# Loading the real weights of one spectral mode in eight pieces instead of one transfer

## The chip, the cores and the metric

The kernel runs on one core of a Trainium2 chip. The metric is the device time of one execution in microseconds (us), the median of several. The core has five engines that run side by side, each with its own queue of instructions: PE (matmuls, with PEld for its weight loads), DVE (vector work), ACT (scalar work, activations), POOL and SP. Data come from HBM through 16 DMA engines, which all queues share.

## What is computed

A sparse attention is followed by a spectral mix. The second part is where the change lies:

```python
x = attention(q, k, v)                     # (8, 576, 512)
X = np.fft.rfft(x, axis=1)                 # 64 modes of it are kept
Yr = einsum('bmd,mde->bme', Xr, w_r) - einsum('bmd,mde->bme', Xi, w_i)
Yi = einsum('bmd,mde->bme', Xr, w_i) + einsum('bmd,mde->bme', Xi, w_r)
y = np.fft.irfft(Y, n=576, axis=1)
u = x + y
out = u + np.maximum(u @ w_ch, 0.0)
```

`w_r` and `w_i` are (64, 512, 512) in float32, 134 MB together. Every weight is used once, for a batch of 8, so the kernel has to bring all of them in from HBM, and it casts them to float16 on the way.

## The kernel before

**Stages.** The attention runs first, strided heads and then local heads. The Fourier transform of x is a matmul with a table (`dft`). The modes are done in two rounds of 64: `mode(slot, m)` works on one half of the 512 input channels, `half = 1 - slot`: round 0 takes the half of the strided heads, beside the local attention, and round 1 that of the local heads, beside the channel mix of x itself (`turn` and `premix`). `mode` does 16 small matmuls (line 547): the stationary operand is a 128 by 128 block of weights, the moving one 16 columns, 8 batches times real and imaginary. The 128 partitions hold 64 rows of the real weights (partitions 0 to 63) over 64 rows of the imaginary ones (64 to 127), so a mode can't start before both of its parts are in.

**The weights.** `w_fetch` (line 174) loads a pair of modes into one tile `wt` of shape [128, 2, 4, 512]: index 1 is the mode of the pair, and a partition's 4 x 512 values are 4 KB of float16 read from 8 KB of contiguous float32. For most pairs there are two transfers, 64 rows of the real part of both modes and 64 rows of the imaginary part, 512 KB each as written (line 196). For the last two pairs, `i >= 2 * NM - 4`, there is one transfer for each part of each mode, 256 KB (line 199), in the order real of the first, real of the second, imaginary of the first, imaginary of the second. The very last pair, `i == 2 * NM - 2` or 126, holds modes 62 and 63 of round 1. All these transfers are issued from POOL's queue, which also issued the loads of q, k and v at the start. Among those are loads of 72 rows that are split into 64 (lines 227 and 229) and 8 (line 231); line 231 is issued twelve times.

`w_fetch` is called at the end of every odd mode (line 555), when that mode's tile comes free: five buffers of the pool `pw` take turns. POOL does nothing else meanwhile. The framework gives the DMAs of POOL's queue eight semaphores in turn; the next DMA on a semaphore waits until the one before on it has landed.

**The order of work at the end.** The program is written out by hand, engine by engine in the order of the code (`manual_schedule`). Modes 0 to 53 of round 1 have turns and premixes between them (lines 845 to 855). Modes 54 to 63 (line 956) have only a few early matmuls, and then `again(n)`, matmuls whose result nobody uses, that keep PE busy between modes (line 949): four after modes 58 to 61, two after 62 and 63. The sums of modes 62 and 63 leave PSUM together, by the add of line 575 after mode 63. Then come `spec_last(0)` (lines 884 and 886, the channel mix of the last 16 modes), three more `again`, `spec_out` on ACT and DVE (lines 675, 677, 678; helper line 260), and the loop over 36 output units: `v_rows` and `u_rows` with the inverse transform (line 688), a ReLU on ACT (line 907), adds on POOL (line 909) and DVE (line 926), and the stores, mostly from SP's queue.

Of the kernel before, what the change touches and what calls it, by code (L numbers as in the profile page):

```python
# [19 lines left out]
NM = 64  # L20
# [59 lines left out]
def kernel(  # L80
# [10 lines left out]
    nc = tc.nc  # L91
# [82 lines left out]
    def w_fetch(n=1):  # L174
        for _ in range(n):
            i = len(w_tiles)
            if i >= 2 * NM:
                return
            half, m = 1 - i // NM, i % NM
            if i // 2 in GUEST:  # L180
                wt = big.tile([128, 2, 4, DM], F16, tag=GUEST[i // 2], name="wt")
            else:
                wt = pw.tile([128, 2, 4, DM], F16, tag="w", name="wt")
            for ri, src in enumerate((moe_w_r, moe_w_i)):
                dst = wt[ds(64 * ri, 64)]
                rows = src[m : m + 2, ds(256 * half, 256), :].rearrange(
                    "m (p c) e -> p m (c e)", c=4
                )
                dst = dst.rearrange("p m c e -> p m (c e)")


                ones = range(2)
                if ri and not m:
                    ones = [1]
                elif i < 2 * NM - 4:
                    nc.gpsimd.dma_start(dst, rows)  # L196
                    continue
                for j in ones:
                    nc.gpsimd.dma_start(dst[:, j], rows[:, j])
            w_tiles.extend((wt[:, 0], wt[:, 1]))  # L200

    def w_ch_fetch():
# [333 lines left out]
    def mode(slot, m):  # L536
# [17 lines left out]
        if m % 2 and (slot or m // 2 not in GUEST):  # L554
            w_fetch()
# [145 lines left out]
    const_load(nc.sync, "cMl", "cFl", "cA")  # L701
    load_str(2, 2)
    w_fetch()

    def str_front(b):
# [39 lines left out]
    for b in range(B):  # L745
        if b in (1, 3):
            load_str(b + 3, 2)
        load_loc(*[(), (), (), (), (0,), (1, 2), (3,), (4, 5)][b])
        w_fetch([2, 1, 1, 1, 1, 1, 0, 0][b])
        front = str_front(b + 1) if b + 1 < B else loc_front(0)  # L750
        for t in range(6):
            str_scores(b, t)
            if b > 0:
                if t < 2:
                    str_values(b - 1, 4 + t)
                elif t == 2:
                    dft(b - 1, 1)
            if t >= 2:
                str_values(b, t - 2)
            for w in front[SPLIT[t] : SPLIT[t + 1]]:  # L760
                w()
        if b == 1:
            nc.vector.memset(PL[:, 0:PS0], 0.0)
# [62 lines left out]
    for b in range(B + 1):  # L826
        for t in range(5):
            if b > 0:
                work.append(lambda b=b, t=t: premix(b - 1, t))
            if b < B and t < 4:  # L830
                half, cp = ((1, 0), (1, 1), (0, 0), (0, 1))[t]
# [181 lines left out]
```

## Time and profile before

| What | us |
|---|---|
| median of 3 runs | 434.96 |
| the runs | 434.02 to 435.61 |
| the profiled execution, one of the three | 435.61 |
| its span, from the first to the last instruction | 433.8 |

| Engine | busy us | share of the span |
|---|---|---|
| PE | 338.7 | 78% |
| PEld | 244.0 | 56% |
| DVE | 215.1 | 50% |
| ACT | 188.1 | 43% |
| POOL | 128.9 | 30% |

The page cuts the span into 40 slices of 10.8 us and gives the busy share of each in tenths. PEclk is the clock that PE was granted in tenths of full speed; DMA is the mean busy share of the 16 DMA engines. A list of queues says how many packets and bytes each moved. The chain of waits follows the work back from the last instruction to whatever released it. "issue" is time in which an engine waited for nothing that the profile shows. In the timeline a line has start and duration, engine, source line, operation, tiles and count, and in brackets how long the engine had been idle before and what ended that. The granted clock of the whole execution was 0.83.

By the list of DMA issues, a 512 KB transfer of weights lands 18.9 us (real) or 19.4 us (imaginary) after its issue in the median, and a 256 KB one 14.7 or 13.4 us after; a load of 8 rows by line 231 (64 KB, two packets a row) 11.5 to 12.2 us after.

### The profile page before, as it was taken

The page shows a single profiled execution, that of the slowest core. Times are in us where ns is not written, and L with a number is a line of the kernel's source. Part 1 is how long each engine was busy: PE and PEld are TensorE (multiplying, and loading weights), DVE is VectorE, ACT ScalarE, POOL GpSimd, SP SyncE. Part 2 cuts the span into 40 slices and gives each one's busy share as a digit, 9 for nine tenths or more (in the row PEclk, how much of TensorE's full clock was granted, in tenths as well). Part 3 has the DMA queues.
Part 4 walks back from the last instruction along what each step waited for, and adds up shares of the span by engine and source line. Part 5 has one row for each costly group of instructions (what it writes and reads, how often), then busy time and mean ns, then how long its engine had stood idle before and what let it go on. Part 6 is the DMA issues. An engine that isn't in the chain of part 4 may idle for free.

```text
span 433.8 us, 12099 instructions
## 1 busy us (share of the span) xinstructions
PE 338.7 (78%) x5307; PEld 244.0 (56%) x5307; DVE 215.1 (50%) x466; ACT 188.1 (43%) x353; POOL 128.9 (30%) x208
## 2 busy tenths in 40 slices
PE   1986888779886887889794566698669698977994
PEld 1865776657764665667663344465446465643441
DVE  2888678744523243342511033455346366503895
ACT  1686678635543435445340401133115122602892
POOL 6522332323232222222222222222222221200983
PEclk9999899869967659676855559868798899988999
DMA  8999999999999999999999999999999999991687
GB/s 178 212 213 213 215 212 212 212 210 213 215 212 214 213 214 213 213 214 214 213 213 213 213 213 215 213 213 215 213 213 213 214 213 213 214 179 29 260 331 275
DMA packets 28996, 92.18 MB, mean 212 GB/s; under 512 B 4048, under 2 KB 5072, under 8 KB 28944
## 3 DMA queue, kind: packets, MB, share of 16 engines
q0 software_dynamic: 24704, 81.28, 94.3%
q1 hardware_dynamic: 3440, 9.46, 5.8%
q10 hardware_dynamic: 800, 0.67, 0.6%
q8 instruction: 42, 0.69, 0.6%
q14 instruction: 10, 0.08, 0.0%
HBM read 163.22 MB, written 9.44 MB: 398 GB/s over the span
## 4 chain that ended last, share of the span: by engine, by line
DMA 69%; PE 18%; DVE 6%; ACT 3%; issue 2%; POOL 1%; DVEq 0%; POOLq 0%
DMA wt<-in_moe_w_i_dram 51%; DMA wt<-in_moe_w_r_dram 8%; DMA ring<-in_q_dram 5%; DMA w_ch<-in_moe_w_ch_dram 5%; DVE xb L250 2%; DVE kz L292 2%; PE y L547 2%; PE v L688 2%; PE u L688 2%; PE v L894 2%; PE sc L514 1%; ACT X L260 1%; DVE rec L249 1%; PE tp L395 1%; PE sc L353 1%
## 5 line engine op out<-in xcount | busy, mean ns | idle before, releaser
L547 PE MATMUL y<-X,wt 128*128 128x16 f16 (+1 forms) x2048 | 82.8, 192 | 59.5 <-DMA wt<-in_moe_w_i_dram 58.1
L547 PEld LDWEIGHTS <-wt 128*128 128x128 f16 (+1 forms) x2048 | 73.1, 103 | 75.4 <-issue 68.3
L196 POOL DMA_DIRECT2D wt<-in_moe_w_r_dram x62 | 36.4, 587 | 139.2 <-PE y L547 66.0
L196 POOL DMA_DIRECT2D wt<-in_moe_w_i_dram x60 | 35.2, 587 | 73.0 <-DMA wt<-in_moe_w_i_dram 60.2
L654 ACT ACTIVATE v<-sc 128x512 f16<-128x512 f32 x32 | 19.1, 596 | 68.4 <-PE sc L645 68.3
L471 ACT ACTIVATE PL<-sc 128x480 f16<-128x480 f32 (+1 forms) x48 | 27.7, 579 | 47.6 <-PE sc L457 46.9
L645 PE MATMUL sc<-w_cp,xT 128*128 128x512 f16 (+1 forms) x160 | 47.4, 424 | 0.0
L655 DVE COPY xo<-tp 128x512 f16<-128x512 f16 x32 | 22.1, 692 | 36.7 <-PE tp L653 36.4
L250 DVE TENSOR_TENSOR xb<-av,rec 90x256 f16<-90x256 f32 (+2 forms) x80 | 36.0, 450 | 2.8
L249 DVE RECIPROCAL rec<-av 90x4 f32<-90x4 f32 (+2 forms) x80 | 14.7, 183 | 45.3 <-PE av L486 33.9
L402 DVE COPY qT<-tp 128x576 f16<-128x576 f16 x16 | 12.0, 758 | 40.1 <-PE tp L395 37.2
L260 ACT ACTIVATE v<-tp 128x640 f16<-128x640 f16 (+1 forms) x24 | 19.4, 807 | 24.0 <-PE tp L429 21.1
L395 PE MATMUL tp<-cI_s,ring 64*64 64x64 f16 x864 | 26.4, 211 | 1.6 <-issue 0.8
L360 ACT ACTIVATE PL<-sc 90x360 f16<-90x360 f32 (+1 forms) x48 | 22.7, 490 | 6.2 <-PE sc L353 5.3
L926 DVE TENSOR_TENSOR osb<-u,rl 128x512 f32<-128x512 f32 x36 | 23.6, 689 | 3.3 <-ACT rl L907 1.7
L395 PEld LDWEIGHTS <-ring 64*64 64x64 f16 x864 | 20.7, 123 | 6.8 <-issue 3.6
L441 PE MATMUL sc<-cMl_s,cI_s 128*128 128x480 f16 (+1 forms) x48 | 23.0, 478 | 1.6 <-ACT X L260 1.6
L909 POOL TENSOR_TENSOR rl<-rl,xo 128x512 f32<-128x512 f32 x16 | 18.3, 1155 | 18.9 <-ACT rl L907 18.6
L457 PE MATMUL sc<-qT,kz 128*128 128x160 f16 (+1 forms) x160 | 23.4, 275 | 0.5 <-issue 0.5
L457 PEld LDWEIGHTS <-kz 128*128 128x128 f16 x160 | 16.8, 119 | 10.8 <-issue 8.1
L907 ACT ACTIVATE rl<-v 128x512 f32<-128x512 f32 x36 | 20.4, 597 | 4.9 <-PE v L688 4.2
L285 PE MATMUL tp<-cI_s,ring 72*128 72x72 f16 x256 | 15.1, 206 | 9.5 <-DMA ring<-in_v_dram 8.0
(103 smaller groups left out, 655.5 us busy)
## 6 DMA issues: line engine op xcount, KB each, us to landing
wt<-in_moe_w_r_dram POOLq DMA_DIRECT2D x62, 512.0 KB, 18.9
wt<-in_moe_w_i_dram POOLq DMA_DIRECT2D x60, 512.0 KB, 19.4
out_dram<-osb SPq DMA_DIRECT2D x14, 512.0 KB, 2.7
ring<-in_v_dram POOLq DMA_DIRECT2D x8, 288.0 KB, 13.4
ring<-in_q_dram POOLq DMA_DIRECT2D x8, 288.0 KB, 13.6
ring<-in_k_dram POOLq DMA_DIRECT2D x8, 288.0 KB, 13.0
ring<-in_v_dram POOLq DMA_DIRECT2D x3, 512.0 KB, 15.1
ring<-in_q_dram POOLq DMA_DIRECT2D x3, 512.0 KB, 14.8
```

The lines of the kernel that those rows point to most:

```text
L196: nc.gpsimd.dma_start(dst, rows)
L250: nc.vector.tensor_tensor(out=dst, in0=val.rearrange("p h (q c) -> p h c q", c=4), in1=rec[0:n, 0:pieces] .to_broadcast((n, pieces, 64)) . ...
L260: nc.scalar.activation(out=out, in_=in_, func=ACTF.Copy)
L360: nc.scalar.activation(out=PS[0:n, ds(POFF[t], 4 * n)], in_=scp[0:n, 0 : 4 * n], func=ACTF.Exp, scale=SCALE,)
L395: nc.tensor.transpose(tp[ds(64 * hp, 64), ds(64 * i, 64)], qn[ds(64 * hp, 64), ds(64 * (9 * g + i), 64)], idn[ds(64 * hp, 64), ds(64 * hp, ...
L441: nc.tensor.matmul(scp[:, 0 : n * times].rearrange("p (h x) -> p h x", h=times), idn, mask_rows("cMl", n, times), start=True, stop=False,)
L457: nc.tensor.matmul(scp[:, ds(col, n)], kzs[par][:, hp, ds(s0, 128)], qTs[par][:, ds(s0, n)], start=False, stop=(i == len(todo) - 1),)
L471: nc.scalar.activation(out=dst, in_=src, func=ACTF.Exp, scale=SCALE)
L547: nc.tensor.matmul(yv[:, mi, e, :], wt[pr, XC[c], ds(128 * e, 128)], Xh[half][pr, c, :, :, m], start=(c == 0), stop=(c == 3),)
L645: nc.tensor.matmul(vp[pr, :], xT[:, ch, cols], w_chs["cp"][:, ch, :], start=(ch == 0), stop=(ch == 3),)
L655: nc.vector.tensor_copy(out=xo[pr].rearrange("p (h q c) -> p h q c", h=2, c=4), in_=tp[pr, 0:512].rearrange("p (h c q) -> p h q c", h=2, c=4),
L926: nc.vector.tensor_tensor(out=osb[:, t % 2, :], in0=up, in1=rls[b, t][:, t % 2, :], op=AluOp.add)
```

## The change

Only `w_fetch` changes, and in it only the last pair, modes 62 and 63 of round 1. Before, it was loaded by four transfers of 256 KB: real 62, real 63, imaginary 62, imaginary 63. Now there are eleven: the real part of mode 62 is cut into eight transfers of 8 rows (32 KB each), and the order is imaginary 62, three pieces of real 62, real 63, three pieces, imaginary 63, the last two pieces. The bytes, the tile and the places in it are the same, and so are all the matmuls and their order. All eleven are still issued from POOL's queue.

```diff
                 for j in ones:
-                    nc.gpsimd.dma_start(dst[:, j], rows[:, j])
+                    if i < 2 * NM - 2:
+                        nc.gpsimd.dma_start(dst[:, j], rows[:, j])
+            if i == 2 * NM - 2:
+
+
+                real = [(wt[a : a + 8, 0], moe_w_r, 0, ds(a, 8)) for a in range(0, 64, 8)]
+                re1 = [(wt[0:64, 1], moe_w_r, 1, ds(0, 64))]
+                im0, im1 = [
+                    [(wt[64:128, j], moe_w_i, j, ds(0, 64))] for j in range(2)
+                ]
+                for d, src, j, p in (
+                    im0 + real[0:3] + re1 + real[3:6] + im1 + real[6:8]
+                ):
+                    nc.gpsimd.dma_start(
+                        d,
+                        src[m + j, ds(256 * half, 256), :].rearrange(
+                            "(p c) e -> p c e", c=4
+                        )[p],
+                    )
             w_tiles.extend((wt[:, 0], wt[:, 1]))
```

## The prediction

> **What bounds the kernel now.** I read the page first. Times are in us from the span's start.
>
> ```profile
> PEclk9999899869967659676855559868798899988999
> DMA  8999999999999999999999999999999999991687
> ...
> q0 software_dynamic: 24704, 81.28, 94.3%
> ...
> q8 instruction: 42, 0.69, 0.6%
> ...
> DMA 69%; PE 18%; DVE 6%; ACT 3%; issue 2%; POOL 1%; DVEq 0%; POOLq 0%
> ```
>
> The reader is to see that the 16 DMA engines are at 90% or more in almost every slice up to about 385 us, and that the chain of waits is 69% DMA. The weights, on POOL's queue (q0), set the time until the last one lands; after that stands a tail of matmuls. So the change touches the one place where the two stretches meet. Next, the chain around that place:
>
> ```profile
> 364.40 19.38 DMA wt<-in_moe_w_i_dram
> 383.78 0.28 issue
> 384.06 9.63 DMA wt<-in_moe_w_i_dram
> 393.69 0.14 issue
> 393.83 0.64 PE y L547 x16
> 394.47 0.50 PE v L951 x2
> 394.97 1.77 PE y L886 x4
> ```
>
> A transfer issued at 364.40 lands at 383.78, and 0.28 later the last one is issued. By the semaphore numbers in the trace POOL keeps eight transfers in flight: each issue waits for the landing of the one eight before it. The last lands at 393.69, mode 63 starts 0.14 later, and the tail follows. Third, the timeline of POOL and PE there:
>
> ```profile
> 376.91 0.52 POOL L199 DMA_DIRECT2D wt<-in_moe_w_r_dram  x1 [2.17 <-DMA wt<-in_moe_w_r_dram]
> 379.09 0.52 POOL L199 DMA_DIRECT2D wt<-in_moe_w_r_dram  x1 [1.66 <-DMA wt<-in_moe_w_i_dram]
> 381.54 0.52 POOL L199 DMA_DIRECT2D wt<-in_moe_w_i_dram  x1 [1.94 <-DMA wt<-in_moe_w_r_dram]
> 384.06 0.52 POOL L199 DMA_DIRECT2D wt<-in_moe_w_i_dram  x1 [2.01 <-DMA wt<-in_moe_w_i_dram]
> ...
> 392.58 0.64 PE L547 MATMUL y<-X,wt 128*128 128x16 f16 x16 [1.69 <-DMA wt<-in_moe_w_i_dram]
> ...
> 393.83 0.64 PE L547 MATMUL y<-X,wt 128*128 128x16 f16 x16 [0.17 <-DMA wt<-in_moe_w_i_dram]
> ```
>
> The four POOL lines are the transfers of the last pair, in the order real 62, real 63, imaginary 62, imaginary 63. Mode 62 starts at 392.58, when the third has landed (392.44); mode 63 at 393.83, after the fourth. Mode 62 is thus done under the last transfer. Last, the windows of 3.41 us (columns: PE, PEld, DVE, ACT, POOL busy, clock, DMA share, GB/s):
>
> ```profile
> 384.46:387.87 3.41, 3.41 (x28) 1.48 (x25) 0.00 (x0) 0.00 (x0) 0.12 (x1) 0.50 0.97 189
> 387.87:391.28 3.41, 3.02 (x42) 1.69 (x40) 0.56 (x1) 0.00 (x0) 0.00 (x0) 1.00 0.54 106
> 391.28:394.70 3.42, 1.95 (x36) 1.21 (x36) 0.20 (x1) 0.00 (x0) 0.00 (x0) 1.00 0.18 36
> 394.70:398.11 3.41, 3.41 (x12) 1.46 (x12) 0.99 (x4) 0.37 (x1) 0.00 (x0) 0.50 0.02 5
> ```
>
> Two things count. DMA falls to half its rate at about 388: the packet records, chained by their starts, show eight engines done between 387.0 and 388.9 and eight between 392.0 and 393.4. Each engine gets the same bytes, but the 42 code fetches of 16 KB (q8, 0.89 to 1.23 us each, durations that repeat every eight) fit eight engines only: 42/8 x 0.95 us is 5 us, the gap. And the clock was halved from 394.70 to 398.11, where the tail begins.
>
> **The change, part by part.** Number the eleven transfers of the last pair: 1 imaginary 62; 2, 3, 4 pieces of real 62; 5 real 63; 6, 7, 8 pieces; 9 imaginary 63; 10, 11 the last two pieces.
>
> *Bytes on each engine: 0.* A 256 KB transfer of 64 rows puts four packets of 4 KB on each engine (0.305 us start to start) and a 4-byte marker (0.021): 1.24 us. For a transfer of 8 rows the nearest row is line 231's, at the start of the kernel: in the packet records of 37 to 63 us it puts packets on eight engines and only markers on the other eight, and the next such transfer takes the other eight, with 64-row transfers between, also from one batch to the next. So eight pieces give each engine four packets, as the one transfer did. The slow eight are not relieved. Added are markers of seven transfers, one or two each: 0.15 to 0.3 us.
>
> The Trainium skill ("DMA: Bandwidth & Descriptors", Bandwidth) speaks against the change: it calls transfers under 64 KB descriptor-dominated and gives 0.95 us for 64 KB. By it eight pieces would take about 7 us of the engines' time, an estimate, and the kernel would lose some 5 us. The rows here have full 4 KB packets at 0.305 us whether the transfer has 8 rows or 64, so I go by the rows.
>
> *Issues on POOL: seven more at 0.52 to 0.61 us (lines 199 and 231), and later.* Numbers 1 to 4 go out where the four did: 376.91, 379.09, 381.54, 384.06. Numbers 5 to 8 wait for the landings of the pair before, in the landing records 385.00, 386.19, 387.43 and 388.73: plus 0.28, 385.28 to 389.01. Number 9 waits for number 1 (in the place of the first of before, which landed at 390.14): 390.42, against 384.06 for the last of before. Numbers 10 and 11 follow at about 390.94 and 391.46. Nothing else is on POOL's queue before its add at 401.71, ten us of cover; the SP and ACT queues are not touched.
>
> *When the last lands.* A busy engine has the same packets as before: 393.69 plus the markers, 393.85 to 394.0, if it is never starved. It nearly is: the landing comes 0.33 after the last marker (393.36 to 393.69), so it ends number 1 at 389.8, and numbers 2 to 8 are 3 or 4 packets of pieces, four of number 5 and markers, 2.3 us: 392.1. And number 9's packets come 1.2 us or more after its issue (the last of before: issued 384.06, first packet on an empty engine at 385.28), so from 391.6. The eight engines that were ahead are empty by then. On those the last transfer of before landed at 387.33 to 387.59, that is 3.27 to 3.53 after its issue: number 9 lands there at 393.7 to 393.95, and one piece with markers (0.35) on top makes 394.05 to 394.3. I take **394.2, 0.5 late**. The other end is the kernel's first load on empty engines, issued at 1.24 and landed at 6.38, 5.14 us: 390.42 + 5.14 + 0.35 is 395.9, 2.2 late. That one ran beside the loads of the constants, which 390 us has none of, so I stay near the first. The lower end is 0.15 late.
>
> *Mode 62 loses its cover: 1.1 to 1.4 us.* Its last pieces are now the last to land, so it starts at 394.2 + 0.14 = 394.34, and the two fillers of line 951, mode 63, its fillers, the add of line 575 and all of lines 884 and 886 queue behind it on PE. From mode 62 to mode 63 it was 1.25, of which 0.17 was the wait: 1.08 at full clock. In a halved window the fillers take 0.43 each and not 0.22, so up to 1.4. Mode 63 starts at 395.4 to 395.7: 1.6 to 1.9 late. The wait on eight semaphores and not two costs nothing: the older ones are passed while the last transfer flies.
>
> *The clock gives some back.* PE idles from 390.9 to 394.3, so a halved window follows as before; if it again ends at 398.11, less of the tail falls into it. Line 886 starts at about 396.9, runs three matmuls at 0.43 and the fourth at full clock, ends at about 398.5; ACT 0.37 and DVE 0.42 as before; line 688 starts near 399.4 against 398.40: 1.0 late. If the window moves along with the work nothing comes back: 1.9. The rest of the tail is the same.
>
> The Trainium skill ("TensorE: Matmul & The Clock Gate", Part 1) says the window of 3413 ns is free-running; the stretches here, all multiples of 3.41, agree, but that it stands elsewhere in another execution no row of one trace can show.
>
> **Sum.** Between 1.0 and 1.9; I take **+1.25 us**. The profiled execution took 435.61 (span 433.8 and 1.8 around it), so it would give 436.9; it was the slowest of three, and on the median of 434.96 it is **436.2 us**.
>
> **The rivals.**
> *Empty engines (slower, one mechanism).* Number 9's issue now hangs on number 1's landing, and if the refill behaves like the kernel's first load, the last landing is 1.1 to 1.7 later than I take: 437.3 to 437.9. For: eight engines are empty for 2 us or more before number 9 comes. Against: the 3.27 us row, which is the same kind of refill. It decides once issue to landing is over 4.2 us.
> *The pieces do not spread as I read them.* If all eight went to the slow eight engines, these get eight packets and not four: 4 x 0.305 is 1.2 more, 437.4. If all went to the eight that are ahead, the slow ones end 1.2 earlier, but number 11, issued at 391.46, can't land before 391.46 + 3.27 - 3 x 0.305 = 393.8, and mode 62 still follows: 435.9. Against both: the alternation in the packet records.
> *Nothing lost.* The landing stays at 393.8 and the halved window falls so that the tail runs at full clock earlier: 434.3 to 435.5. For: the three runs before spread over 1.6 us. Against: mode 62's 1.08 has no cover left.
>
> **How the numbers follow.** Half a per cent, 2.2 us, is about what can be told from no change: bounds 432.8 and 437.1. My forecast 0.60, all but 0.05 of it within; empty engines 0.20, slower; the pieces elsewhere 0.08, half of it slower; nothing lost 0.12, of which 0.05 goes to a gain for which I have no mechanism. That makes faster 0.05, same 0.66, slower 0.29. The forecast's own range is 435.6 to 436.9; to hold 8 in 10 it reaches down to 434.7 and up through the empty engines to 438.0.
>
> **What would show it.** In the changed kernel: mode 62 and mode 63 together after one last DMA, about 1.1 to 1.4 apart, with a wait of over 3 us before mode 62; POOL's ninth issue of the pair near 390.4; a last landing of 394.0 to 394.3; the eleven issues' bytes the same. I am wrong if number 9 is issued much earlier, if mode 62 still starts before the last landing, if the last landing is past 395, or if the slow eight engines end before 393.

## The result, and the profile after

| | median us | runs |
|---|---|---|
| before | 434.94 | 434.02 to 436.41, 6 runs |
| changed | 438.28 | 437.75 to 439.86, 6 runs |
| ratio | 1.0078 | 95% interval 1.0054 to 1.0102 |

The changed kernel is slower by 3.3 us. In a second group of runs it was 438.33 against 435.43, a ratio of 1.0064 (1.0040 to 1.0088). The profiled execution took 438.41, its span 436.5, 2.7 more than before. Two executions in the experiments (605.70 us in run 2, 507.19 us in run 9) were slow ones and are not in the ratios. The code above `w_fetch`'s end keeps its lines; below it every line number is 18 higher (547 is 565, 951 is 969, 886 is 904, 688 is 706), and the eleven transfers have line 212. The kernels of the experiments are made from the changed one, and their lines differ from it by up to two; those of 11 and 12 are made from the one before.

The page of the changed kernel, the two rows of the 40 slices that show where it differs:

```profile
PEclk9998989969985556886975558889579599966999
DMA  8999999999999999999999999999999999980687
```

For 35 slices the DMA engines are as busy as before. The 36th has 8 where before it had 9, and the 37th 0 where it had 1. The chain of waits of the changed kernel, from the first transfer of the last pair on:

```profile
376.90 13.09 DMA wt<-in_moe_w_i_dram
389.98 0.28 issue
390.26 0.90 POOL wt L212 x2
391.16 0.12 issue
391.29 3.52 DMA wt<-in_moe_w_r_dram
394.80 0.24 issue
395.05 0.64 PE y L565 x16
395.68 0.85 PE v L969 x2
396.54 0.47 PE y L565 x16
397.01 0.85 PE v L969 x2
397.86 1.71 PE y L904 x4
```

Before, this chain ran from a landing at 383.78 through one transfer of 9.63 us to 393.69. Now it runs through the landing of the pair's own first transfer (389.98), three issues and the flight of the eleventh: 394.80. Then both modes and both pairs of fillers stand on the chain, where only mode 63 stood. The timeline of the changed kernel:

```profile
390.26 0.53 POOL L212 DMA_DIRECT2D wt<-in_moe_w_i_dram  x1 [0.75 <-DMA wt<-in_moe_w_i_dram]
...
395.05 0.64 PE L565 MATMUL y<-X,wt 128*128 128x16 f16 x16 [3.10 <-DMA wt<-in_moe_w_r_dram]
...
396.33 0.68 PE L565 MATMUL y<-X,wt 128*128 128x16 f16 x16
...
397.66 1.91 PE L904 MATMUL y<-w_ch,YT 128*128 128x512 f16 x4
...
401.11 0.81 PE L706 MATMUL v<-zz,cA_s 128*128 128x512 f16 x3
```

PE stands idle for 3.10 us, and the first inverse transform of the tail (line 706) starts at 401.11, against 398.40 before: all of the 2.7 us is there by then. The windows show the clock (columns as in the prediction):

```profile
383.63:387.04 3.41, 3.13 (x38) 1.77 (x39) 0.00 (x0) 0.00 (x0) 1.53 (x3) 0.50 0.78 144
387.04:390.45 3.41, 3.41 (x25) 1.45 (x24) 0.00 (x0) 0.00 (x0) 1.25 (x4) 0.50 0.86 154
390.45:393.87 3.42, 1.49 (x21) 0.76 (x19) 0.56 (x1) 0.00 (x0) 1.36 (x3) 1.00 0.68 109
393.87:397.28 3.41, 2.23 (x36) 1.38 (x36) 0.23 (x1) 0.00 (x0) 0.00 (x0) 0.50 0.01 1
397.28:400.69 3.41, 3.41 (x13) 1.45 (x12) 0.74 (x3) 0.37 (x1) 0.00 (x0) 0.50 0.02 5
400.69:404.10 3.41, 3.05 (x13) 1.15 (x12) 2.16 (x5) 2.53 (x5) 0.00 (x0) 1.00 0.08 33
```

Two halved windows in a row, 393.87 to 400.69, where before there was one, 394.70 to 398.11. A window with 1.49 us of PE work is followed by a halved one, and so is the next, with 2.23; so is the first, with 3.13 us at half clock.

A second profile of the changed kernel (run 10) has one halved window there and not two, 396.12 to 399.53. PE in it:

```profile
396.07 0.64 PE L565 MATMUL y<-X,wt 128*128 128x16 f16 x16 [4.65 <-DMA wt<-in_moe_w_r_dram]
...
397.35 0.68 PE L565 MATMUL y<-X,wt 128*128 128x16 f16 x16
...
401.06 0.81 PE L706 MATMUL v<-zz,cA_s 128*128 128x512 f16 x3
```

From mode 63 to line 706 it took 3.71 us, 4.78 in the first profile and 4.57 before.

Two stretches of the end are enough to tell the kernels apart: from the last landing of the pair before (modes 60 and 61) to the last landing of all, and from that to the first matmul of the inverse transforms. All profiles in one table; "over before" is the ratio of the comparison times 435, its interval in parentheses:

| kernel | landing to landing, us | last landing to inverse transforms, us | over before, us |
|---|---|---|---|
| before | 4.96 | 4.71 | |
| changed | 6.08 | 6.31 | 3.4 (2.3 to 4.4) |
| changed, again | 6.25 | 5.32 | 2.8 (1.7 to 3.8) |
| order alone | 5.02 | 5.44 | 1.6 (0.9 to 2.3) |
| four pieces of 16 | 4.70 | 5.30 | 2.0 (1.3 to 2.7) |
| four pieces of 8, one of 32 | 5.01 | 5.77 | 1.3 (0.5 to 2.1) |
| late, no piece of 8 | 6.19 | 6.55 | 3.2 (1.9 to 4.4) |
| pieces last | 6.37 | 6.63 | 3.3 (2.0 to 4.7) |
| pieces are mode 63's | 6.33 | 4.75 | 2.1 (1.3 to 2.8) |
| three pieces first | 5.62 | 6.51 | 1.9 (1.0 to 2.8) |
| changed, 14 fillers | 5.85 | 5.60 | 2.2 (1.0 to 3.3) |
| changed, 19 fillers | 6.22 | 4.14 | 1.3 (0.7 to 1.8) |
| before, 9 fillers | 4.96 | 3.12 | -0.7 (-1.5 to -0.0) |
| before, 9 fillers, again | 4.95 | 3.12 | -0.7 (-1.2 to -0.2) |

The first column comes from the landing records (the times at which each of the 16 engines reported a transfer, without the engine's number), the second from the timeline. The landing of the pair before lies between 388.72 and 389.77 in these profiles, which is why the count starts there. The 4.70 of the four pieces of 16 is too small, as run 2 tells.

### The profile page after: what moved, and what is told of

Read it like the earlier page. It is cut to its first block, busy times and chain, and to the rows that moved or that the text cites. A ratio compares the mean times of both kernels' runs of the same rounds, so it can differ in the third digit from the quotient of the medians.

```text
span 436.5 us, 12110 instructions
## 1 busy us (share of the span) xinstructions
PE 342.9 (79%) x5307; PEld 245.1 (56%) x5307; DVE 215.3 (49%) x466; ACT 188.4 (43%) x353; POOL 133.0 (30%) x215
## 4 chain that ended last, share of the span: by engine, by line
DMA 81%; PE 13%; issue 2%; DVE 1%; ACT 1%; POOL 1%; DVEq 0%; POOLq 0%
DMA wt<-in_moe_w_i_dram 49%; DMA wt<-in_moe_w_r_dram 9%; DMA ring<-in_v_dram 8%; DMA ring<-in_k_dram 6%; DMA w_ch<-in_moe_w_ch_dram 5%; DMA ring<-in_q_dram 4%; PE v L706 2%; PE u L706 2%; PE sc L663 2%; PE v L912 2%; PE y L565 1%; PE v L969 1%; PE y L904 1%; PE u L933 1%; PE tp L303 1%
## 5 line engine op out<-in xcount | busy, mean ns | idle before, releaser
L663 PE MATMUL sc<-w_cp,xT 128*128 128x512 f16 (+1 forms) x160 | 51.5, 454 | 0.0
L278 ACT ACTIVATE kz<-tp 64x360 f16<-64x360 f16 (+1 forms) x32 | 19.0, 594 | 8.9 <-PE tp L413 7.5
L663 PEld LDWEIGHTS <-xT 128*128 128x128 f16 (+1 forms) x160 | 14.8, 111 | 13.9 <-issue 6.9
```

The source lines that it names most:

```text
L278: nc.scalar.activation(out=out, in_=in_, func=ACTF.Copy)
L663: nc.tensor.matmul(vp[pr, :], xT[:, ch, cols], w_chs["cp"][:, ch, :], start=(ch == 0), stop=(ch == 3),)
```

## The experiments

**1. The order alone.** Four transfers of 64 rows, but real 62 last.

```diff
-    im0 + real[0:3] + re1 + real[3:6] + im1 + real[6:8]
+    im0 + re1 + im1 + re0
```

> Order alone: four transfers of 64 rows as before, but imaginary 62, real 63, imaginary 63, real 62. Theory 'same engines' (each piece of 8 rows goes to the same eight DMA engines, of which one or two are among the late ones; this made the last landing 1.1 us late, and mode 62's loss of cover made the rest): the last landing stays within 0.2 of 393.7, mode 62 starts after it, mode 63 1.1 to 1.3 later, and the time is 1.3 to 2.0 us over before, so some half of the loss of 3.3. Rival 'order alone' (the pieces cost nothing, all of the loss is mode 62 and the halved clock after a long idle stretch): 2.7 us or more over before.

Measured: 437.06 against 435.18, ratio 1.0037 (1.0021 to 1.0054). The timeline of this kernel:

```profile
394.24 0.64 PE L565 MATMUL y<-X,wt 128*128 128x16 f16 x16 [3.22 <-DMA wt<-in_moe_w_r_dram]
...
395.15 0.64 PE L565 MATMUL y<-X,wt 128*128 128x16 f16 x16
```

The last landing, 394.10, is where it was before (5.02 after the landing of the pair before, against 4.96), mode 62 waits for it, and mode 63 is 0.91 behind, less than the 1.1 to 1.3 expected. Half of the loss is here without a single piece: the order does it. The rival, that the order is all of it, is out by its interval.

**2. Four pieces of 16 rows.** The interleaving is kept, with seven transfers.

```diff
+    real = [part(0, 0, a, 16)[0] for a in range(0, 64, 16)]
-    im0 + real[0:3] + re1 + real[3:6] + im1 + real[6:8]
+    im0 + real[0:2] + re1 + real[2:3] + im1 + real[3:4]
```

> Real 62 in four pieces of 16 rows in the same interleaving: imaginary 62, two pieces, real 63, one piece, imaginary 63, one piece. Seven transfers, so none waits for a landing of the same pair. 'Same engines': 16 rows put one packet on each engine, so the last landing is 393.6 to 394.0 and the time as in the run with the order alone, 1.3 to 2.2 over before. Rival 'pieces cost in themselves' (small transfers between large ones slow the engines): last landing 394.5 or more, time 2.5 to 3.3 over before.

Measured: ratio 1.0047 (1.0031 to 1.0063), 2.0 us, last landing 394.40. That is higher than I had allowed for. Landing to landing it is only 4.70, but that number is too small: one engine was 0.87 behind the next already at the landing of the pair before (389.70 and 388.83), and still 0.62 behind at the last (394.40 and 393.78). From the first issue of the pair (377.01) the next engine took 16.77, and with the order alone 16.78 (377.26 to 394.04). So apart from that one engine, whose delay was there already, small transfers between large ones cost next to nothing in themselves. (`part(j, ri, a, n)` makes the transfer of n rows from row a, of part ri of mode j.)

**3. Half of it in pieces of 8.** Four pieces of 8 rows and one of 32: eight transfers, so that none waits for a landing of its own pair.

```diff
+    real = [part(0, 0, a, 8)[0] for a in range(0, 32, 8)] + part(0, 0, 32, 32)
-    im0 + real[0:3] + re1 + real[3:6] + im1 + real[6:8]
+    im0 + real[0:2] + re1 + real[2:4] + im1 + real[4:5]
```

> Four pieces of 8 rows and one of 32 rows, last: eight transfers, none waits for a landing of the same pair. 'Same engines': the eight engines get 4 + 2 packets of real 62 and not 4, so 2 x 0.305 = 0.6 more: last landing 394.2 to 394.5. Rival 'late issue' (the delay came from the ninth to eleventh transfers being issued after 390): last landing 393.6 to 394.0. If pieces of 8 rows alternate between the halves, as I had read from the loads at the start: 393.6 to 394.0 too.

Measured: ratio 1.0031 (1.0012 to 1.0049), landing to landing 5.01 (the last at 394.39, in a profile that issued the pair 0.65 later, at 377.56 and not 376.91). The theory of the same engines had asked for 0.6 more; there is none. If some engines had two packets more here, none of them was the last to end; the landing records don't say which engine is which.

**4. Late issue without a piece of 8.** Real 62 and real 63 in four pieces of 16 rows each, so ten transfers, imaginary 63 the ninth.

```diff
+    real = [part(0, 0, a, 16)[0] for a in range(0, 64, 16)]
+    more = [part(1, 0, a, 16)[0] for a in range(0, 64, 16)]
-    im0 + real[0:3] + re1 + real[3:6] + im1 + real[6:8]
+    im0 + real[0:3] + more[0:4] + im1 + real[3:4]
```

> Ten transfers without one of 8 rows: imaginary 62, three pieces of 16 rows of real 62, real 63 in four pieces of 16 rows, imaginary 63, the last piece of real 62. Imaginary 63 is the ninth, issued near 390.3 as in the changed kernel. 'Same engines': every engine has the bytes of before, so the last landing is 393.9 to 394.3, set by the late issue, and the time 1.6 to 2.4 over before. Rival 'late issue' makes the whole delay: 394.6 to 395.0, time 2.9 to 3.4 over before.

Measured: ratio 1.0073 (1.0044 to 1.0102), as slow as the changed kernel. Its chain of waits:

```profile
377.77 13.03 DMA wt<-in_moe_w_i_dram
390.80 0.28 issue
391.08 0.48 POOL wt L214
391.56 0.04 issue
391.60 4.18 DMA wt<-in_moe_w_r_dram
395.78 0.09 issue
```

The same shape as in the changed kernel: the ninth transfer waits for the first to land (390.80), is issued at 391.08, and by the landing records reaches the sixteen engines between 394.33 and 395.51, 3.25 to 4.43 us after its issue. By 393.04 every engine had reported the eighth. From those sixteen reports to those of the ninth, each in order of time, it is 2.1 to 2.5 us, where four packets take 1.24: the engines stood without data in between. Landing to landing 6.19 with not one piece of 8 rows: late issue alone is enough for the whole delay. Whether it makes that of the changed kernel this run can't say.

**5. All eight pieces, last.**

```diff
-    im0 + real[0:3] + re1 + real[3:6] + im1 + real[6:8]
+    im0 + re1 + im1 + real[0:8]
```

> All eight pieces of 8 rows of the changed kernel, but after the large transfers: imaginary 62, real 63, imaginary 63, then the pieces. Only three small pieces are issued late, and the engines have large transfers to work on until then. Theory 'late issue' (the ninth transfer waits for the first to land, the engines run dry and the refill takes 3.2 to 4.4 us): the last landing comes 3.5 to 3.9 us after the first transfer of the pair has landed (3.55 before, 4.82 in the changed kernel), and the time is that of the run with the order alone, 1.5 to 2.1 over before. Rival 'same engines' (eight engines get all the pieces, 1.2 us more of work): 4.7 or more, and 2.7 to 3.4 over before.

Measured: ratio 1.0077 (1.0047 to 1.0107), 5.15 us from the first landing, and so a miss of 'late issue' as I had put it; both numbers lie where 'same engines' had put them. One reason is in the landing records: the eleventh transfer waits for the third, a large one, to land (393.05), goes out at 393.33 and lands at 395.70, 2.37 later. So the run doesn't tell the theories apart, but the landings of this last piece show something else, us for the sixteen engines:

```
394.73 394.75 394.76 394.77 394.78 394.79 394.81 394.83
395.53 395.56 395.59 395.60 395.61 395.67 395.68 395.70
```

Eight engines report 0.8 us before the others: a piece of 8 rows has data for eight engines, and the other eight only report. The packet records, chained by their starts, say more: two engines take a packet of each of the first seven pieces, one after the other, 0.325 apart (one from 391.89 to 393.84, the other from 391.93 to 393.88). Pieces that alternated between the halves would not do that.

**6. The pieces belong to mode 63.** The transfers of the changed kernel with the parts of the two modes exchanged, so that mode 62 is complete with the fifth.

```diff
+    real = [part(1, 0, a, 8)[0] for a in range(0, 64, 8)]
-    im0 + real[0:3] + re1 + real[3:6] + im1 + real[6:8]
+    im0 + real[0:3] + re0 + real[3:6] + im1 + real[6:8]
```

> The transfers of the changed kernel with the parts of modes 62 and 63 exchanged: the pieces are the real part of mode 63, and the real part of 62 goes whole in fifth place, so that mode 62 is done before the last landing. Theory 'two causes' (late landing 1.1 to 1.4, mode 62's cover 1.3 to 1.6): the late landing stays, mode 62 starts 1 us or more before it, mode 63 about 0.2 after it, and the time is 1.0 to 1.9 over before. Rival 'the landing is all' : 2.7 or more over before.

Measured: ratio 1.0048 (1.0030 to 1.0065), 2.1 us, a little above what I had written. The timeline of this kernel:

```profile
392.70 0.65 PE L566 MATMUL y<-X,wt 128*128 128x16 f16 x16
...
396.34 0.64 PE L566 MATMUL y<-X,wt 128*128 128x16 f16 x16 [2.55 <-DMA wt<-in_moe_w_r_dram]
```

Mode 62 is done 2.7 us before the last landing. The late landing stays (6.33), the stretch after it is that of before (4.75 and 4.71). With the first experiment this is the split from both sides: the order without the late landing 1.6, the late landing without the order 2.1.

**7. and 8. Fillers in the changed kernel.** After mode 61, 14 and then 19 matmuls of `again` and not 4.

```diff
-    again(0 if m < NM - 6 else 4 if m < NM - 2 else 2)
+    again(0 if m < NM - 6 else 4 if m < NM - 3 else 19 if m < NM - 2 else 2)
```

> The changed kernel with 14 filler matmuls and not 4 after mode 61, so that PE is busy while it waits for the last landing. Theory 'the halved clock is part of the loss' (the long wait leaves the tail from mode 62 to the first inverse transforms at half clock): the clock in the 3.4 us after mode 62 is mostly 1.0, fillers between the modes take 0.22 each, and the time falls by 0.7 to 1.8 against the changed kernel. Rival (clock no part of it): within 0.4 of the changed kernel.

> The changed kernel with 19 fillers after mode 61, enough for the whole wait of 3.75 us and 0.4 more at full clock. 'The halved clock is part of the loss': no halved window between mode 62 and the inverse transforms, time 0.8 to 1.6 below the changed kernel, 1.7 to 2.5 over before. Rival (the fillers hold up mode 62 as much as the clock gives): within 0.4 of the changed kernel.

Measured: with 14, 437.95 and ratio 1.0050 (1.0023 to 1.0076), not told apart from the changed kernel, where I had expected 0.7 to 1.8 less. The fillers ended at 393.86, mode 62 came at 395.21, and the clock was halved from 396.51 to 399.92 all the same. With 19, 436.91 and ratio 1.0029 (1.0015 to 1.0042): 1.4 us under the median of the changed kernel beside it and 1.5 over that of before, a little better than expected. Its windows:

```profile
391.82:395.23 3.41, 2.99 (x14) 1.18 (x12) 0.00 (x0) 0.00 (x0) 0.76 (x2) 1.00 0.65 100
395.23:398.64 3.41, 2.66 (x40) 1.65 (x41) 0.29 (x1) 0.00 (x0) 0.00 (x0) 1.00 0.03 5
398.64:402.05 3.41, 3.29 (x19) 1.43 (x18) 2.06 (x5) 2.08 (x5) 0.00 (x0) 1.00 0.01 2
```

Full clock throughout, and the stretch after the last landing shrinks to 4.14, from 6.31 and 5.32 in the two profiles of the changed kernel, although the landing is as late as ever (6.22). The halved clock is about half of the loss, 1.4 of 2.9.

**9. Three pieces first.** So the ninth to eleventh wait for small transfers that land early, and mode 62 is still the last to be complete.

```diff
-    im0 + real[0:3] + re1 + real[3:6] + im1 + real[6:8]
+    real[0:3] + im0 + re1 + im1 + real[3:8]
```

> All eight pieces of 8 rows, in another order: three pieces, imaginary 62, real 63, imaginary 63, five pieces. The ninth to eleventh transfers now wait for the landings of the first three, which are small and land before 389.5, so they are issued by 390.6 while the engines still have large transfers to work on; mode 62 is still the last to be complete. Theory 'late issue': from the landing of the pair before to the last landing it is 4.9 to 5.3 us (4.96 before, 5.02 with the order alone, 6.08 in the changed kernel), and the time is 1.4 to 2.1 over before. Rival 'same engines' (eight engines have four packets more of 0.305 us): 5.6 to 6.2, and 2.4 to 3.3 over before.

Measured: ratio 1.0043 (1.0023 to 1.0064), landing to landing 5.62, between the two theories and at the lower edge of the rival's; the time, 1.9 over, is in the range of 'late issue'. The chain of waits of this kernel and then the landing records of its last five pieces, us, the latest engine and the one before it:

```profile
389.27 0.28 issue
389.55 1.32 POOL wt L213 x3
390.87 0.18 issue
391.05 3.84 DMA wt<-in_moe_w_r_dram
394.89 0.24 issue
```

```
latest engine     393.60 393.91 394.23 394.56 394.89
the one before it 393.27 393.50 393.82 394.15 394.47
twelfth of 16     392.90 393.06 393.22 393.63 393.79
```

The last issue is at 391.05, and the latest engine has work until 393.26, the landing of imaginary 63, so it is not starved. Yet it takes one packet more at every piece, 0.31 to 0.34 us each, five times in a row, and the one before it at the last three. In the packet records these are five packets on one engine, at 392.93, 393.25, 393.58, 393.90 and 394.23, each followed by its marker. Pieces that alternated between the halves would have stepped it only every other time. So 'same engines' is true as well, and worth about 0.6 here.

**10. The changed kernel again.**

> The changed kernel once more beside the others on the same chip: 3.0 to 3.6 over before by all theories. Its profile gives a second look at the last landing: 'late issue' has all sixteen engines ending within 0.5 us of each other and 3.2 to 4.4 us after the ninth issue; 'same engines' has one or two engines ending 0.3 to 0.6 after the rest, with steps of 0.32 at every piece.

Measured: 438.33 against 435.43, just under the 3.0 expected, landing to landing 6.25. Both signs are there: fifteen engines end between 394.97 and 395.32, 4.0 to 4.3 us after the ninth issue, and one 0.42 after them at 395.74. The steps of 0.33 at each of the last two pieces (395.08, 395.41, 395.74) are its own.

**11. and 12. Fillers in the kernel before.** Nine after mode 61 and not four, run twice.

```diff
-    again(0 if m < NM - 6 else 4 if m < NM - 2 else 2)
+    again(0 if m < NM - 6 else 4 if m < NM - 3 else 9 if m < NM - 2 else 2)
```

> The kernel before with 9 fillers and not 4 after mode 61. If the halved clock costs the kernel before too (394.70 to 398.11 in its profile), the time falls by 0.5 to 1.5 below before. Rival: the fillers fall into a halved window themselves and hold up modes 62 and 63: same or up to 1 slower.

> The kernel before with 9 fillers and not 4 after mode 61, once more with more rounds, since its interval nearly reached no change. If the halved window behind the last landing costs the kernel before in most executions, it is 0.5 to 1.2 below before again and its runs lie closer together than those of before. Rival (chance, or a chip that happened to suit it): within 0.3 of before.

Measured: 434.58 against 435.34, ratio 0.9983 (0.9966 to 0.9999), then 434.77 against 435.48, ratio 0.9983 (0.9972 to 0.9995). This is 0.7 us below the kernel before, and its runs lie within 0.7 and 1.2 us of each other where those of before beside them spread over 2.7 and 2.4. The windows of the first:

```profile
389.04:392.46 3.42, 3.14 (x29) 1.46 (x27) 0.56 (x1) 0.00 (x0) 0.00 (x0) 1.00 0.53 105
392.46:395.87 3.41, 2.59 (x39) 1.48 (x40) 0.29 (x1) 0.00 (x0) 0.00 (x0) 1.00 0.09 18
395.87:399.28 3.41, 3.37 (x19) 1.53 (x18) 1.86 (x4) 1.88 (x4) 0.00 (x0) 1.00 0.04 7
```

No halved window, and the stretch after the last landing is 3.12, not 4.71; in the second run's profile it is 3.12 too.

## Why the prediction was wrong

The time, 438.28, lies above the range (434.7 to 438.0), and I had held a time within half a per cent of before likeliest. The sum had the right terms. Two of its steps failed: that the pieces add no bytes to any engine, which put the last landing too early, and that the clock gives something back, which held in one profile and not in the other. Term by term:

| term | predicted | first profile | second profile |
|---|---|---|---|
| last landing | 0.5 late | 1.1 late (6.08 and not 4.96) | 1.3 late (6.25) |
| mode 62 loses its cover | 1.1 to 1.4 | 1.4 (mode 62 to mode 63 1.28, and 0.24 and not 0.14 from landing to matmul) | 1.5 (1.28, and 0.33) |
| clock | 0.6 to 0.9 back | 0.2 more lost | 0.9 back |
| sum | 1.0 to 1.9, taken as 1.25 | 2.7 | 1.9 |

The second profile stands 0.8 later as a whole, already when the last pair is issued (377.67 and not 376.90), and so do those of runs 8 and 9 on the same chip (377.70 and 377.47); this is not the change. Of the 3.3 between the first medians, 0.6 stands in none of these terms; most of it is that the profiled run before took 435.61, 0.67 above its median, and the changed one 0.13 above. What makes that is open.

*Bytes on each engine: 0.* This step failed. I read the alternation from loads of 8 rows that have two pieces of 4 KB a row, and it does hold for those. The pieces of the change have one, and they go to the same eight engines: runs 5 and 9 show it packet by packet, and the latest engine steps by 0.31 to 0.34 at every piece. In the first profile of the changed kernel this set the last landing. The engine that ends last has its packets there without a gap: the piece number 8 at 392.26, four of number 9 from 392.58 on, the last two pieces at 393.82 and 394.14. From there on it was never without data, and it landed at 394.80; the other fifteen landed by 394.45. The rival that said so had been given 0.08.

The Trainium skill ("DMA: Bandwidth & Descriptors", Why a DMA increments its semaphore by 16 and not by 1) has both cases: a round-robin cursor where fewer than 16 engines take part, and an exception by which some copies from POOL's queue put the partitions, divided by 16 and rounded up, on each engine from the first on. Eight rows would by that always be on the first eight engines. The steps here agree with the exception, the loads at the start with the cursor; that it is this exception no run here shows.

*Issues on POOL.* Right: the ninth was issued at 390.26 (predicted 390.42), the eleventh at 391.29 (391.46).

*When the last lands.* The mechanism, a refill of empty engines because the ninth transfer hangs on the first's landing, was right for the engines that did run empty, and its size wrong. I took 3.27 to 3.53 us from issue to landing from four engines that were quickest. Over all sixteen it is 3.2 to 3.9 in the changed kernel, 3.3 to 4.1 in its second profile and 3.25 to 4.43 in run 4. I should have taken the slowest engine, as the last landing is the slowest. Late issue alone (run 4) and the same engines alone (run 9) give 1.2 and 0.6 more landing to landing, both together 1.1 and 1.3 in the two profiles of the changed kernel: they overlap, since an engine that has more packets waits less. In the first profile the latest engine did not wait at all; in the second the latest landing of the ninth comes 2.06 after that of the eighth, where four packets take 1.24, so it waited too. How a single execution splits between them stays open: of the five profiles with a large ninth transfer and pieces of 8 rows, the last engine stood 0.35 to 0.62 behind the next in four, and 0.02 behind in run 7.

*Mode 62 loses its cover.* Right to its upper end. Runs 1 and 6 show it from both sides. I had called the longer wait list on PE free; from landing to matmul it is 0.24 and 0.33, not 0.14. That the list makes it is not shown: in runs 2 and 4, where mode 62 waits for five transfers and not two, it is 0.09.

*The clock gives some back.* I let the halved window end where it ended before and the tail run past it. In the first profile a second one followed and took 0.2 more; in the second there was one, and 0.9 came back, as I had it. So the same kernel loses or gains 1.1 us here from one execution to another, and the sum should have carried that as a range. The prediction had the other case ("If the window moves along with the work nothing comes back: 1.9.") and I leant the other way. How much PE work lifts the clock is no single number. In the 14 profiles, from 382 to 402 us, a window at full clock with 2.07 us of PE work or less was followed by a halved one, and one with 2.13 or more by a full one; a halved window was followed by a full one only where PE was busy in all of its 3.41 us, and 3.13 were not enough. Earlier in these profiles the cases overlap: windows at full clock with 1.63 to 2.63 us went either way. Runs 8 and 11 show the size of the stretch after the landing at full clock: 4.14 against 5.32 and 6.31 in the two profiles of the changed kernel, 3.12 against 4.71 in the kernel before.

*The rivals.* 'Empty engines' was nearest in the time (437.3 to 437.9), with the pieces not spreading as its companion. The landing it asked for (395.3 to 395.9) is later than the 394.80 measured, and than the 395.74 of the second profile less the 0.8 by which that one stood later; and the ninth's 3.90 and 4.07 us from issue to landing stay under the 4.2 that were to decide for it. I kept them apart, at 0.20 and 0.08, though they were to come together. 'Nothing lost' is out.

## What to carry to other kernels

Where a queue keeps a fixed number of transfers in flight, cutting the last ones into pieces leaves fewer bytes in flight: count which landing each issue waits for, and what the engines still have to do by then. The last data to land should belong to the last work, and nothing else should wait for it. When PE idles for a DMA before a chain of matmuls, price the chain at half clock, and try fillers that last as long as the wait; here they were the only change that came out below the kernel before.

## What was not expected of the hardware

Nine fillers, 2 us of work whose result nobody uses, made the kernel before faster by 0.7 us and its runs steadier, though its last landing came no earlier (394.21 in its profile, 393.69 before).

A piece without data for an engine still delays that engine's report: in the second profile of the changed kernel the latest engine reports the first transfer at 390.72 and the next two, both pieces, at 390.88 and 391.05. These steps are half of the 0.32 of a packet, and more than the 0.02 that a marker takes in the packet records. The data behind it are not held up so long: in the first profile a marker of number 1 stands at 390.302, six 4-byte packets follow it from 390.324 on, and the next packet of 4 KB starts at 390.358.
